# Narrower value columns, fewer GpSimd masks, a rearranged start and new scheduling durations in a fused attention and SwiGLU kernel

## The chip, the cores and the metric

The kernel runs on one core of one Trainium2 chip. The metric is the device time of one launch in microseconds; several launches are timed and the median is quoted. In the profile PE is TensorE's matmuls, PEld its weight loads (they overlap PE), DVE is VectorE, ACT is ScalarE, POOL is GpSimd and SP is the engine that issues most DMAs. "L380" is line 380 of that kernel. Line numbers differ between kernels, so the text says each time what the line does.

## The reference, cut to what matters

```python
# q, k, v: (8 batches, 8 heads, 576, 64) float32; tau = 0.02
scores = q @ k.T / 8
thresh = max(scores, axis=-1) - tau
scores = where(scores >= thresh, scores, -1e9)
attn   = softmax(scores)
x      = (attn @ v) laid out as 4608 tokens x 512
xn     = x / rms(x) * rms_g
out    = (silu(xn @ w_gate) * (xn @ w_val)) @ w_out      # 512 -> 1536 -> 512
```

The outer shapes make 144 attention steps: 36 chunks of 128 queries (32 from one batch each, 4 built from the 64 left-over queries of two batches) times 4 pairs of heads. A step computes 128 x 576 scores for two heads.

## The kernel before

One Python function builds a list of operations with their dependencies, engine and an assumed duration. A list scheduler then sorts them, and each engine executes its own list strictly in that order.

```python
COST = dict(s_main=1080.0, ..., av_main=600.0, ..., mask_g=800.0, take_g=1400.0, ..., xn=400.0, ...)   # ns
```

A step goes through these stages (cuts marked with dots):

```python
# 1. scores: TensorE, fp32, two heads side by side into PSUM
# 2. per head, VectorE: copy to SBUF and take the row minimum (scores are negated)
nc.vector.tensor_tensor_reduce(out=ssb[a][:, h], in0=s_ps[h][:, 448:1024], in1=zrow, ..., accum_out=mx[m][:, h:h + 1])
# 3. GpSimd: threshold = minimum + tau, a 128 x 2 instruction
nc.gpsimd.tensor_scalar(out=nth[m], in0=mx[m], scalar1=tau, ...)
# 4. per head one of two ways, by WAYS[s % len(WAYS)]
#    "p": ScalarE alone: a steep leaky ReLU that throws out what is over the threshold, then exp
nc.scalar.activation(out=ssb[a][:, h], in_=ssb[a][:, h], func=PRELU, scale=-1.0, bias=nth[m][:, h:h + 1], ...)
nc.scalar.activation(out=wsb[s % NW][:, h], in_=ssb[a][:, h], func=AF.Exp)
#    "g": exp on ScalarE, mask and multiply on GpSimd
nc.scalar.activation(out=esb[es], in_=ssb[a][:, h], func=AF.Exp, scale=-1.0, bias=nth[m][:, h:h + 1])
nc.gpsimd.tensor_scalar(out=wsb[s % NW][:, h], in0=ssb[a][:, h], scalar1=nth[m][:, h:h + 1], op0=ALU.is_le, ...)
nc.gpsimd.tensor_tensor(out=wsb[s % NW][:, h], in0=wsb[s % NW][:, h], in1=esb[es], op=ALU.mult)
# 5. transpose the 128 x 1152 weights by DMA (fp16)
nc.sync.dma_start_transpose(out=wt[s % NWT], in_=wsb[s % NW]...)
# 6. attention times value ("AV"): 10 matmuls; the moving side is 64 values and 64 ones
#    (a strided view over the value tile), and column 64 is the softmax sum
nc.tensor.matmul(ot[:, cs], w[:, 4 * h + j], v_rhs(b % 2, p, 5 * h + j), start=(j == 0), stop=(j == 4))
```

In this kernel `FIRST = 16` and `WAYS = ("pg",)`: the first 16 steps use ScalarE alone, and from there every second head is masked on GpSimd.

The FFN works on groups of up to four chunks. Its gate and value weights come in 24 pieces of 128 x 512, are multiplied by `rms_g` and cast to fp16 on GpSimd, and the first FFN matmul waits for all 24:

```python
for d in range(4):                                   # 128 rows
    for w_dram, w_sb in ((moe_w_gate, wg), (moe_w_val, wv)):
        for c in range(DFF // 512):                  # 512 columns
            ...
            nc.gpsimd.tensor_scalar(out=w_sb[d][:, 512 * c:512 * (c + 1)], in0=stage[slot],
                                    scalar1=rmsg[:, d:d + 1], scalar2=None, op0=ALU.mult)
...
g = add("PE", mm, pr, xops + w_done + ..., gmm, ring="R")     # w_done: all 24 casts
```

Of the kernel before, what the change touches and what calls it, by code (L numbers as in the profile page):

```python
# [13 lines left out]
SEM = 150.0  # L14
COST = dict(
    s_main=1080.0, s_virt=2160.0, tr4=480.0, av_main=600.0, av_virt=800.0, ffn4=216.0,
    ttr=850.0, evac_qk=620.0, evac_kt=420.0, prelu=740.0, exp0=660.0, exp1=750.0, mask_d=910.0, mask_g=800.0, take_g=1400.0,
    rz=120.0, xmul=400.0, sq=720.0, xn=400.0, pool_tiny=380.0, pool_dma=1300.0, sp=70.0,
    gate=0.0,
# [3 lines left out]
class Op:  # L23
    __slots__ = ("eng", "cost", "prio", "deps", "fn", "ring", "frees", "slot", "end", "start", "dma", "opens")

    def __init__(self, eng, cost, prio, deps, fn, ring=None, frees=None, dma=0.0):
        self.eng, self.cost, self.prio, self.fn = eng, cost, prio, fn
        self.deps = [d for d in deps if d is not None]
        self.ring, self.frees, self.dma = ring, frees, dma
        self.slot = self.end = self.start = None  # L30
        self.opens = ()


def order_ops(ops, ring_sizes):
# [20 lines left out]
    while len(out) < len(ops):  # L55
        best = None
        for e, lst in pending.items():
            if not lst:
                continue
            t0 = eng_free[e]  # L60
            cand = None
            for i in lst:
                o = ops[i]
                t = max(t0, ready_at[i])
                if o.ring is not None:
                    if not ring_free[o.ring]:
                        continue
                    t = max(t, min(ring_free[o.ring])[0])
                k = (t, o.prio, i)
                if cand is None or k < cand:  # L70
                    cand = k
            if cand is not None and (best is None or cand < best[0]):
                best = (cand, e)
# [3 lines left out]
        if o.ring is not None:  # L77
            got = min(ring_free[o.ring])
            ring_free[o.ring].remove(got)
            o.slot = got[1]  # L80
# [6 lines left out]
        if o.frees is not None:  # L87
            ring_free[o.frees.ring].append((o.end + SEM, o.frees.slot))
# [14 lines left out]
def kernel(  # L103
# [32 lines left out]
    id32 = sb("id32", [128, 128])  # L136
    zrow = sb("zrow", [128, S], FP16)
# [5 lines left out]
    qn = [sb(f"qn{i}", [128, 4, 2, D]) for i in range(2)]  # L143
    kn = [sb(f"kn{i}", [128, 4, 2, D]) for i in range(2)]
    qtl = [sb(f"qtl{i}", [128, H, D]) for i in range(2)]
    ktl = [sb(f"ktl{i}", [128, H, D]) for i in range(2)]
    qT = [[sb(f"qT{i}_{p}", [128, MAIN]) for p in range(NP)] for i in range(2)]
    kT = [[sb(f"kT{i}_{p}", [128, MAIN]) for p in range(NP)] for i in range(2)]
    kTt = [sb(f"kTt{i}", [128, NP, TAIL]) for i in range(2)]
    qTv = [sb(f"qTv{i}", [128, NP, 128]) for i in range(2)]  # L150
    va = [sb(f"va{i}", [128, NP, 13, D], FP16) for i in range(2)]

    def v_rhs(i, p, j):
        kind = {4: 11, 5: 12}.get(j, 10)
        a = va[i][:, p, j:j + 2]
        return bass.AP(tensor=a.tensor, offset=a.offset, ap=[a.ap[0], [D * (kind - j), 2], a.ap[2]])

# [21 lines left out]
    sl = [sb(f"sl{i}", [128, 512]) for i in range(NT_)]  # L179
    NHF = 18  # L180
# [37 lines left out]
    n_load = {"q": 0, "k": 0}  # L218
    tr_of = {"q": [], "k": []}
    k_ready = {}  # L220
    kt_ready = {}
    q_ready = {}
# [4 lines left out]
    def setup():  # L227
        o_id = add("POOL", 2000.0, -100, [], lambda o: make_identity(nc, id32))

        def consts(o):  # L230
            nc.vector.memset(zrow, 0.0)
            nc.vector.memset(mhalf, -0.5)

        def vconst(o):
            for i in range(2):
                nc.vector.memset(va[i][:, :, 10:13], 1.0)
                for j in (4, 11):
                    nc.vector.memset(va[i][64:128, :, j], 0.0)
                for j in (5, 12):
                    nc.vector.memset(va[i][0:64, :, j], 0.0)  # L240

        o_c = add("DVE", 300.0, -100, [], consts)
# [8 lines left out]
    def emit_qk(b, p, which, prio):  # L251
        nat = (qn if which == "q" else kn)
        dst = (qT if which == "q" else kT)[b % 2][p]
        src = (q if which == "q" else k)[b, 2 * p:2 * p + 2, 0:MAIN]
        n = n_load[which]
        n_load[which] += 1
        slot = n % 2
        before = [tr_of[which][n - 2]] if n >= 2 else []

        def load(o):  # L260
            for h in range(2):
                nc.sync.dma_start(out=nat[slot][:, :, h], in_=src[h].rearrange("(si sc) d -> si sc d", sc=4))

        def tr(o):
            for sc in range(4):
                nc.tensor.transpose(ring[o.slot][:, 128 * sc:128 * (sc + 1)], nat[slot][:, sc].rearrange("s h d -> s (h d)"), id32)  # L266

        lo = gated(add("SP", 70.0, prio - 3, before, load, dma=1500.0), prio - 3)
        t = add("PE", COST["tr4"], prio, [lo, o_id] + last_s.get((which, b - 2, p), []), tr, ring="R")
        tr_of[which].append(t)  # L270

        def ev(o):
            nc.scalar.activation(out=dst, in_=ring[t.slot], func=AF.Copy, scale=-0.125 if which == "q" else 1.0)  # L273

        e = add("ACT", COST["evac_qk"], prio, [t], ev, frees=t)
        (q_ready if which == "q" else k_ready)[b, p] = e

    def emit_tail_load(b, prio):
        i, e = divmod(b, 2)
        before = [x for x in tail_load.get(("use", i - 2), [])]  # L280
        for which, dst, src in (("q", qtl, q), ("k", ktl, k)):
# [3 lines left out]
            tail_load[which, b] = gated(add("SP", 70.0, prio - 3, before, load, dma=800.0), prio - 3)  # L285

    def emit_k_tail(b, prio):
        i, e = divmod(b, 2)

        def tr(o):  # L290
            for p in range(NP):
                nc.tensor.transpose(
                    ring[o.slot][:, 64 * p:64 * (p + 1)],
# [6 lines left out]
        def ev(o):  # L300
            nc.scalar.copy(out=kTt[b % 2], in_=ring[t.slot][:, 0:64 * NP].rearrange("p (a n) -> p a n", n=TAIL))

        kt_ready[b] = add("ACT", COST["evac_kt"], prio, [t], ev, frees=t)
        tail_load.setdefault(("use", i), []).append(t)

    def emit_q_tail(i, prio):
        def tr(o):
            for p in range(NP):
                nc.tensor.transpose(
                    ring[o.slot][:, 128 * p:128 * (p + 1)],  # L310
# [6 lines left out]
        def ev(o):  # L317
            nc.scalar.activation(out=qTv[i % 2], in_=ring[t.slot].rearrange("p (a n) -> p a n", n=128),
                                 func=AF.Copy, scale=-0.125)

        qv_ready[i] = add("ACT", COST["evac_qk"], prio, [t], ev, frees=t)
        tail_load.setdefault(("use", i), []).append(t)

    def emit_v(b, prio):
        t = va[b % 2]
        hv = v[b].rearrange("(a e) s d -> e s a d", e=2)
        main = v[b, :, 0:MAIN].rearrange("(a e) (si sc) d -> e si a (sc d)", e=2, sc=4)
# [8 lines left out]
        def run(lo, hi, p, j, n):  # L336
            return t[lo:hi, p:p + 2, j:j + n].rearrange("s a j d -> s a (j d)")

        for g in range(NP // 2):
            prs = [2 * g, 2 * g + 1]  # L340
            put(prs, 4 * g, run(64, 128, 2 * g, 0, 4), main[0, 0:64, prs[0]:prs[0] + 2], 360.0)
            put(prs, 4 * g + 0.1, run(0, 64, 2 * g, 1, 4), main[0, 64:128, prs[0]:prs[0] + 2], 360.0)
            put(prs, 4 * g + 0.2, run(0, 128, 2 * g, 6, 4), main[1, :, prs[0]:prs[0] + 2], 720.0)
            if g == 0:
                allp = list(range(NP))
                put(allp, 0.3, t[0:64, :, 0], hv[0, MAIN:S], 500.0)
                put(allp, 0.4, t[64:128, :, 5], hv[1, MAIN:S], 500.0)

    def emit_batch_inputs(b):
        base = first_step[b - 1] if b else -10  # L350
        emit_tail_load(b, base + (0 if b else 1))
        for p in range(NP):
            pr = base + 3.5 * p + (1.5 if b else 0)
            emit_qk(b, p, "k", pr)
            emit_qk(b, p, "q", pr + 0.1)
            if p == 0:
                emit_k_tail(b, pr + 0.2)
        emit_v(b, base + (5 if b else 0))
        if b % 2:
            emit_q_tail(b // 2, base + 13)  # L360
# [7 lines left out]
    w_dma = {}  # L368

    def emit_s(s):  # L370
        ci, p = steps[s]
        kind, b, c = chunks[ci]
        if kind == "m":
            deps = [q_ready[b, p], k_ready[b, p], kt_ready[b]]

            def fn(o):
                for lo, n, src in ((512, MAIN, kT[b % 2][p]), (448, TAIL, kTt[b % 2][:, p])):
                    for h in range(2):
                        hs = slice(64 * h, 64 * h + 64)
                        nc.tensor.matmul(s_ps[h][:, lo:lo + n], qT[b % 2][p][hs, 128 * c:128 * (c + 1)],  # L380
                                         src[hs], start=True, stop=True)
        else:
            deps = [qv_ready[b]]
            for e in range(2):
                deps += [k_ready[2 * b + e, p], kt_ready[2 * b + e]]
# [12 lines left out]
        if kind == "m":  # L398
            last_s[("q", b, p)] = [o]
            last_s[("k", b, p)] = [o] + ([last_s["k", b, p][0]] if False else [])  # L400
# [7 lines left out]
    def emit_softmax(s, so):  # L408
# [3 lines left out]
        for h in range(2):  # L412
            def ttr(o, h=h):
                nc.vector.tensor_tensor_reduce(  # L414
                    out=ssb[a][:, h], in0=s_ps[h][:, 448:1024], in1=zrow, scale=1.0, scalar=3.0e38,
# [8 lines left out]
        wfree = [w_dma.get(s - NW)]  # L424
        done = []
        for h in range(2):
            way = (WAYS[s % len(WAYS)] if s >= FIRST else "pp")[h]
            if way == "p":
# [7 lines left out]
                pl = add("ACT", COST["prelu"], s + 0.5, [tn], prelu)  # L436
                done.append(add("ACT", COST["exp0"], s + 0.5, [pl] + wfree, ex))
# [34 lines left out]
        def tdma(o):  # L472
            nc.sync.dma_start_transpose(out=wt[s % NWT], in_=wsb[s % NW].rearrange("p h s -> p (h s)"))

        w_dma[s] = add("SP", COST["sp"], s, done + [av_of.get(s - NWT)], tdma, dma=1700.0)

    def emit_av(s):
        ci, p = steps[s]
        kind, b, c = chunks[ci]
        col = (s % 2) * 4 * D  # L480
        w = wt[s % NWT]

        def fn(o):
            for h in range(2):
                cs = slice(col + h * 2 * D, col + (h + 1) * 2 * D)
                if kind == "m":
                    for j in range(5):
                        nc.tensor.matmul(ot[:, cs], w[:, 4 * h + j], v_rhs(b % 2, p, 5 * h + j),  # L488
                                         start=(j == 0), stop=(j == 4))
                else:  # L490
                    for e in range(2):
                        for j in range(5):
                            nc.tensor.matmul(ot[64 * e:64 * e + 64, cs], w[:, 4 * h + j, 64 * e:64 * e + 64],  # L493
                                             v_rhs(e, p, 5 * h + j), start=(j == 0), stop=(j == 4))

        bs = [b] if kind == "m" else [2 * b, 2 * b + 1]
        deps = [w_dma[s]] + [x for bb in bs for x in v_ready[bb, p]]
# [3 lines left out]
        av_of[s] = o  # L501
# [4 lines left out]
    def emit_half(s):  # L506
# [4 lines left out]
        o3 = ot.rearrange("p (h d) -> p h d", d=2 * D)  # L511
# [248 lines left out]
```

## Time and profile before

| | before |
|---|---|
| time, median (all runs beside the changed kernel) | 704.02 us (701.69 to 707.34) |
| span of the profiled run | 699.8 us |
| TensorE, GpSimd, ScalarE, VectorE busy | 92, 76, 65, 61% |
| first FFN matmul starts at | 90.7 us |

I cut the span at two landmarks that can be read from the timeline of TensorE. The first is the start of the scores of step 20, after the first batch and the first left-over chunk; the second is the end of the last scores. This gives a start, a middle and a tail that hold the same attention work in every kernel. (The amount of FFN work ahead of a landmark differs. Counted in matmuls of the full 512 columns, 0.215 us each, 18 lie ahead of the first landmark in the kernel before. Behind the second they are 202.) These are the three stretches of the kernel before; the columns are the stretch, its length, busy us and instruction count of PE, PEld, DVE, ACT and POOL, then granted clock, DMA share and GB/s:

```profile
0.00:99.10 99.10, 72.02 (x455) 47.58 (x455) 39.89 (x116) 61.13 (x102) 63.80 (x79) 0.85 1.02 193
99.10:645.70 546.60, 521.32 (x3953) 305.26 (x3952) 357.05 (x866) 372.32 (x629) 458.20 (x484) 0.98 0.67 123
645.70:699.80 54.10, 48.46 (x463) 35.76 (x459) 31.86 (x102) 21.79 (x58) 7.33 (x9) 1.00 0.21 52
```

In the start TensorE is idle for 27 us, at a granted clock of 0.85, and the DMA engines are full. In the middle TensorE is 95% busy and GpSimd 84%. The chain of waits of the whole span, by engine, has both:

```profile
PE 45%; POOL 29%; issue 8%; DMA 6%; ACT 6%; DVE 4%; SPq 1%; POOLq 0%; DVEq 0%; ACTq 0%
```

### The profile page before, as it was taken

Reading aid. Unit: us, or ns where it says so; the run is one execution under the profiler, and the core shown is the slowest. Engines: PE = TensorE matmul, PEld = TensorE weight load, DVE = VectorE, ACT = ScalarE, POOL = GpSimd, SP = SyncE. Lnnn points to the kernel's source line nnn. Section 1 sums busy time; section 2 is a strip of 40 time slices with the busy share of each in tenths; the row PEclk is TensorE's granted clock in tenths of the full one; section 3 lists DMA queues with packets and bytes.
Section 4 is the critical chain, followed back from the end, with each engine's and each line's share of the span. In section 5 each row is a group of like instructions: output and inputs, shape, how many; then the busy total and the mean of one; then the engine's idle time right before and its main releaser. Section 6 shows DMA issues by size and latency. Waiting matters only on the chain.

```text
span 699.8 us, 13808 instructions
## 1 busy us (share of the span) xinstructions
PE 641.8 (92%) x4864; PEld 388.6 (56%) x4864; DVE 428.8 (61%) x1080; ACT 455.2 (65%) x789; POOL 529.3 (76%) x570
## 2 busy tenths in 40 slices
PE   5787699989899898999999999999999989999997
PEld 3455466756545444555675545555555544556775
DVE  2353465754568645875685784767478656865654
ACT  2867566666767656766776866776677756766443
POOL 3087987599889966898898987899789977887300
PEclk9897889998899999999999999999999999999999
DMA  9899997487686546975897455977596454444410
GB/s 163 172 257 202 214 145 159 76 138 136 139 119 115 98 107 133 145 124 122 171 129 144 91 114 116 162 119 124 118 183 114 85 107 101 78 97 112 82 46 31
DMA packets 290325, 89.00 MB, mean 127 GB/s; under 512 B 272848, under 2 KB 282576, under 8 KB 290256
## 3 DMA queue, kind: packets, MB, share of 16 engines
q1 hardware_dynamic: 275344, 81.83, 59.1%
q0 software_dynamic: 14912, 6.30, 8.7%
q8 instruction: 38, 0.62, 0.4%
q14 instruction: 31, 0.25, 0.1%
HBM read 37.75 MB, written 9.44 MB: 67 GB/s over the span
## 4 chain that ended last, share of the span: by engine, by line
PE 45%; POOL 29%; issue 8%; DMA 6%; ACT 6%; DVE 4%; SPq 1%; POOLq 0%; DVEq 0%; ACTq 0%
POOL wsb L457 13%; PE s_ps L380 12%; POOL wsb L462 8%; PE ring L615 8%; PE ring L576 6%; PE ring L581 6%; DMA wt<-wsb 5%; PE ot L488 5%; POOL nth L421 2%; ACT ssb L430 2%; DVE ssb L414 2%; PE ring L266 2%; PE ot L493 2%; POOL wv L674 2%; ACT wsb L434 1%
## 5 line engine op out<-in xcount | busy, mean ns | idle before, releaser
L414 DVE CUSTOM_DVE_ANT_0 ssb<-s_ps,zrow 128x576 f32<-128x576 f32 x288 | 208.4, 753 | 135.8 <-PE s_ps L380 91.9
L457 POOL TENSOR_SCALAR wsb<-ssb,nth 128x576 f16<-128x576 f32 x128 | 221.6, 1731 | 9.1
L380 PE MATMUL s_ps<-kT,qT 64*128 64x512 f32 x512 | 172.3, 676 | 15.0 <-DVE mx L414 9.9
L462 POOL TENSOR_TENSOR wsb<-wsb,esb 128x576 f16<-128x576 f16 x128 | 163.4, 1277 | 11.3 <-ACT esb L443 1.9
L443 ACT ACTIVATE esb<-ssb,nth 128x576 f16<-128x576 f32 x128 | 98.8, 772 | 95.0 <-POOL nth L421 94.6
L430 ACT ACTIVATE ssb<-ssb,nth 128x576 f32<-128x576 f32 x160 | 121.0, 762 | 12.4 <-POOL nth L421 12.4
L581 PE MATMUL ring<-xnT,wv 128*128 128x512 f16 (+2 forms) x528 | 108.4, 328 | 2.6 <-DVE sl L591 1.8
L488 PE MATMUL ot<-va,wt 128*128 128x128 f16 x1280 | 97.4, 226 | 14.6 <-DMA wt<-wsb 12.0
L434 ACT ACTIVATE wsb<-ssb 128x576 f16<-128x576 f32 x160 | 107.6, 680 | 3.9
L576 PE MATMUL ring<-xnT,wg 128*128 128x512 f16 (+2 forms) x520 | 107.3, 329 | 0.9 <-ACT qT L273 0.7
L588 ACT ACTIVATE th<-ring 128x512 f32<-128x512 f32 (+2 forms) x130 | 63.0, 488 | 57.2 <-PE ring L576 57.0
L488 PEld LDWEIGHTS <-wt 128*128 128x128 f16 x1280 | 80.3, 101 | 34.8 <-DMA wt<-wsb 21.8
L591 DVE SCALAR_TENSOR_TENSOR sl<-th,ring 128x512 f32<-128x512 f32 (+2 forms) x130 | 71.9, 553 | 45.1 <-ACT th L588 43.1
L421 POOL TENSOR_SCALAR nth<-mx 128x2 f32<-128x2 f32 x144 | 34.6, 240 | 81.6 <-DVE mx L414 61.6
L380 PEld LDWEIGHTS s_ps<-kTt,qT 64*128 64x128 f32 x512 | 62.3, 196 | 60.3 <-issue 58.5
L615 PE MATMUL ring<-wo,hf 128*128 128x512 f16 x396 | 90.3, 379 | 0.0
L596 DVE TENSOR_TENSOR hf<-ring,sl 128x512 f16<-128x512 f32 (+2 forms) x132 | 73.7, 558 | 12.1 <-PE ring L581 2.4
L380 PEld LDWEIGHTS s_ps<-kT,qT 64*128 64x128 f32 x512 | 48.8, 194 | 57.3 <-DVE mx L414 26.5
L581 PEld LDWEIGHTS <-wv 128*128 128x128 f16 x624 | 54.6, 98 | 33.4 <-issue 4.6
L576 PEld LDWEIGHTS <-wg 128*128 128x128 f16 x624 | 55.2, 98 | 31.4 <-issue 1.7
L615 PEld LDWEIGHTS <-hf 128*128 128x128 f16 x432 | 40.7, 98 | 44.9 <-issue 0.2
L380 PE MATMUL s_ps<-kTt,qT 64*128 64x64 f32 x512 | 54.0, 252 | 0.0
(50 smaller groups left out, 515.9 us busy)
## 6 DMA issues: line engine op xcount, KB each, us to landing
kn<-in_k_dram SPq DMA_DIRECT2D x64, 128.0 KB, 3.1
qn<-in_q_dram SPq DMA_DIRECT2D x64, 128.0 KB, 3.5
out_dram<-osb SPq DMA_DIRECT2D x32, 256.0 KB, 2.6
th<-in_moe_w_gate_dram SPq DMA_DIRECT2D x12, 256.0 KB, 3.5
sl<-in_moe_w_val_dram SPq DMA_DIRECT2D x12, 256.0 KB, 3.6
wt<-wsb SPq DMA_TRANSPOSE x144, 3.3
va<-in_v_dram POOLq DMA_DIRECT2D x32, 64.0 KB, 4.0
va<-in_v_dram POOLq DMA_DIRECT2D x16, 128.0 KB, 4.5
```

What stands on the lines that cost most here:

```text
L380: nc.tensor.matmul(s_ps[h][:, lo:lo + n], qT[b % 2][p][hs, 128 * c:128 * (c + 1)], src[hs], start=True, stop=True)
L414: nc.vector.tensor_tensor_reduce(out=ssb[a][:, h], in0=s_ps[h][:, 448:1024], in1=zrow, scale=1.0, scalar=3.0e38, op0=ALU.add, op1=ALU.min, ...
L430: nc.scalar.activation(out=ssb[a][:, h], in_=ssb[a][:, h], func=PRELU, scale=-1.0, bias=nth[m][:, h:h + 1], **PRELU_KW)
L434: nc.scalar.activation(out=wsb[s % NW][:, h], in_=ssb[a][:, h], func=AF.Exp)
L443: nc.scalar.activation(out=esb[es], in_=ssb[a][:, h], func=AF.Exp, scale=-1.0, bias=nth[m][:, h:h + 1])
L457: nc.gpsimd.tensor_scalar(out=wsb[s % NW][:, h], in0=ssb[a][:, h], scalar1=nth[m][:, h:h + 1], scalar2=None, op0=ALU.is_le)
L462: nc.gpsimd.tensor_tensor(out=wsb[s % NW][:, h], in0=wsb[s % NW][:, h], in1=esb[es], op=ALU.mult)
L488: nc.tensor.matmul(ot[:, cs], w[:, 4 * h + j], v_rhs(b % 2, p, 5 * h + j), start=(j == 0), stop=(j == 4))
L576: nc.tensor.matmul(ring[o.slot][:, 0:n], wg[d][:, fs], xnT[slot][:, d, 0:n], start=(d == 0), stop=(d == 3))
L581: nc.tensor.matmul(ring[o.slot][:, 0:n], wv[d][:, fs], xnT[slot][:, d, 0:n], start=(d == 0), stop=(d == 3))
L596: nc.vector.tensor_tensor(out=hf[hi][:, 0:n], in0=ring[vv.slot][:, 0:n], in1=sl[i][:, 0:n], op=ALU.mult)
L615: nc.tensor.matmul(ring[o.slot], hf[hs[fc][0]][:, 128 * j:128 * (j + 1)], wo[:, fc], start=(fc == 0), stop=(fc == NFC - 1))
```

## The change

The intent is to give TensorE less to do, to take GpSimd off the path, and to get through the start sooner. The diff, cut to its core (cuts are marked with "..."; helpers for two PSUM slots per operation, renamed tiles, merged q/k tiles, four staging tiles of their own for the weight loads, output weights that no longer wait for casts, and other priorities are left out):

```diff
-    s_main=1080.0, s_virt=2160.0, tr4=480.0, av_main=600.0, av_virt=800.0, ffn4=216.0,
-    ttr=850.0, ..., mask_g=800.0, take_g=1400.0,
+    s_main=1120.0, s_virt=1130.0, tr4=480.0, tr8=560.0, av_main=360.0, av_virt=500.0, ffn4=216.0,
+    ttr=690.0, ..., mask_g=1740.0, take_g=1300.0,
...
-    va = [sb(f"va{i}", [128, NP, 13, D], FP16) for i in range(2)]
+    va = [sb(f"va{i}", [128, NP, 10, D + 1], FP16) for i in range(2)]
...
-            put(prs, 4 * g, run(64, 128, 2 * g, 0, 4), main[0, 0:64, prs[0]:prs[0] + 2], 360.0)
+            put([p], VSTEP[b > 0] * p, t[64:128, p, 0:4, 0:D], main[2 * p, 0:64], 500.0)
...
-                        nc.tensor.matmul(ot[:, cs], w[:, 4 * h + j], v_rhs(b % 2, p, 5 * h + j),
+                        nc.tensor.matmul(ot[:, cs], w[:, 4 * h + j], va[b % 2][:, p, 5 * h + j],
...
+        if s < N_PE:
+            def tr(o):
+                for j in range(9):
+                    nc.tensor.transpose(ring[...], wsb[s % NW][... 128 * j:128 * j + 128], id16)
+            ...                       # and two copies PSUM -> wt on VectorE
+        else:
             nc.sync.dma_start_transpose(out=wt[s % NWT], in_=wsb[s % NW]...)
...
-            nc.vector.tensor_scalar(out=xn[ci % 2], in0=xsb[ci % 2], scalar1=ir[i3], scalar2=None, op0=ALU.mult)
+            nc.gpsimd.tensor_scalar(out=xn[ci % 2], in0=xsb[ci % 2], scalar1=ir[i3], scalar2=1.0,
+                                    op0=ALU.mult, op1=ALU.mult)
...
-    for d in range(4):
-        for w_dram, w_sb in ((moe_w_gate, wg), (moe_w_val, wv)):
-            for c in range(DFF // 512):
+    for c in range(DFF // 512):
+        for d in range(4):
+            for w_dram, w_sb in ((moe_w_gate, wg), (moe_w_val, wv)):
...
-                    nc.gpsimd.tensor_scalar(
+                    nc.vector.tensor_scalar(          # the cast of the weights
...
-FIRST = 16
-WAYS = ("pg",)
+FIRST = 0
+WAYS = ("pg", "pp")
+N_PE = 16
+EVAC = ("ACT", "DVE")                                 # k^T now leaves PSUM by VectorE
```

A value tile now holds 64 values and one column of ones per block, so the loads write rows of 64 values with a gap, where two heads' worth of four blocks went as runs of 256 values before. `WAYS = ("pg", "pp")` masks one head in four on GpSimd, and `N_PE = 16` is the number of first steps whose weights TensorE transposes. An FFN matmul now waits only for the 8 casts of its own column block. Where both heads of a step go the "p" way, one exp covers both.

## The prediction

> **What bounds the kernel now.** I read the page first (engine shares, slices), then one table of five stretches of the span, then the chain that ended last in two of them.
>
> ```profile
> PE 641.8 (92%) x4864; PEld 388.6 (56%) x4864; DVE 428.8 (61%) x1080; ACT 455.2 (65%) x789; POOL 529.3 (76%) x570
> ...
> PE   5787699989899898999999999999999989999997
> ...
> POOL 3087987599889966898898987899789977887300
> PEclk9897889998899999999999999999999999999999
> DMA  9899997487686546975897455977596454444410
> ```
>
> TensorE is the fullest engine, GpSimd the second. The PE row is low only in the first six or seven slices (about 100 us); there DMA is at 9 and the granted clock below full.
>
> The stretches (us, length, busy us and instructions of PE, PEld, DVE, ACT, POOL, then clock, DMA share, GB/s):
>
> ```profile
> 0.00:20.00 20.00, 10.74 (x52) 7.62 (x52) 5.81 (x20) 6.20 (x10) 6.47 (x16) 1.00 1.06 161
> 20.00:100.00 80.00, 62.19 (x406) 40.71 (x408) 34.87 (x98) 55.75 (x95) 58.23 (x63) 0.81 1.01 201
> 100.00:340.00 240.00, 224.09 (x1709) 135.44 (x1706) 148.46 (x372) 159.41 (x274) 201.21 (x214) 0.96 0.70 127
> 340.00:640.00 300.00, 290.62 (x2188) 164.78 (x2188) 202.49 (x479) 208.44 (x348) 251.73 (x266) 1.00 0.65 120
> 640.00:700.00 60.00, 54.16 (x514) 40.05 (x512) 37.16 (x114) 25.45 (x66) 11.69 (x14) 1.00 0.23 56
> ```
>
> So PE is 73% busy to 100 us (72.9 of 100), 93% to 340, 97% to 640, 90% in the tail. A busy PE still counts pipeline ends, so I add the work from start-to-start times of the timeline: scores 1.23 us a step (144 steps, 178 us), FFN matmuls 0.86 us per four of 512 columns and 2.59 us per twelve of the output (280 us in all), the q/k transposes about 32 us, attention-times-value (AV) 56 ns each (below), 1600 of them, 90 us. Sum 580 of 700 us; some 120 us are lost. Before 100 us only about 20 of 144 score steps and five of the twelve column blocks of the first FFN group are done, some 47 us of work, so 53 us are lost there; 13 us go in the tail (47 us of work in 60), and some 55 between 100 and 640.
>
> What takes them is in the chain of 20 to 100 us and of 340 to 400 us:
>
> ```profile
> 43.63 3.11 POOL wv L674 x2
> ...
> 70.86 3.10 POOL wg L674 x2
> ...
> 82.24 3.11 POOL wg L674 x2
> ```
>
> ```profile
> 342.53 0.52 POOL wsb L462
> 343.05 0.85 issue
> 343.90 0.23 POOL nth L421
> 344.22 1.74 POOL wsb L457
> 346.03 1.28 POOL wsb L462
> ```
>
> Early, the threshold (L421) of every step waits in GpSimd's in-order queue behind weight casts (L674, 24 of 1.57 us). Later, in stretches, mask plus multiply plus threshold, 1.74+1.28+0.23 = 3.25 us, are the step's pace; in others (354 to 385 us) the chain is PE alone.
>
> **What the Trainium skill says.**
> (1) "TensorE: Matmul & The Clock Gate", section "Back-to-back issue gap": an isolated warm gap is N/2.4 + 2.5 ns, so 56 ns at N=128, but about 81 ns sustained with weight loads. This trace:
>
> ```profile
> 304.53 0.72 PE L488 MATMUL ot<-va,wt 128*128 128x128 f16 x10
> 305.09 1.03 PE L576 MATMUL ring<-xnT,wg 128*128 128x512 f16 x4
> ```
>
> 0.56 us for ten load-and-matmul pairs, 56 ns: the loads are hidden, the first figure holds here and the second doesn't. At 65 columns the formula gives 29.6 ns; whether loads still hide is not shown.
> (2) "GPSIMD Engine Reference", section "Elementwise — side-by-side cycle accounting": two-input work about 2.6 cycles an element at 1.2 GHz. L462: 1277 ns for 576 is 2.66; it agrees. The mask at 1731 ns (3.6 cycles) is dearer than its one-input figure.
> (3) "SBUF — State Buffer", "shared port pair" among its terms: VectorE in a two-port mode and GpSimd lock one pair exclusively and the loser waits. The normalise on VectorE (L534) has 479/520/1500 ns min/median/max; that spread agrees, and its mean is 819.
> (4) "ScalarE: Activation LUTs", "What ACT_TABLE_LOAD costs": 186 ns + 0.833 ns an element without a pointer operand: 666 ns at 576, the trace has 680; 1146 at 1152.
>
> **The change part by part.**
> *AV with 65 columns.* 1600 matmuls, from 56 ns to somewhere from 30 (stream bound) to 56 (load bound). I choose 36: minus 20 ns x 1600 = 32 us, nearly all between 100 and 640 us where PE is the bound. On the path, about 30 us.
> *Masks on every fourth head.* L457 and L462 fall from 128 to 72: minus 56 x (1.731+1.277) = minus 168 us of GpSimd. ACT: prelu from 160 to 216 (+56 x 0.762 = +43), biased exp from 128 to 72 (-43), 160 exps of 0.68 (109) become 72 of 0.68 and 72 double ones of about 1.15 (132, +23). The k copy out of PSUM goes to DVE (-19). ACT ends near 460 us, no bound.
> *Casts to DVE.* GpSimd minus 37 us; DVE plus 24 x (0.5 to 1.5, as L534) = about 20.
> *Normalise to GpSimd.* Plus 36 x 1.57 (the cast's row, same shape) = at most 56; DVE minus 29.
> *Value loads.* One row of 64 per descriptor, 112 loads for 96: GpSimd plus 16 x 0.67 = 11. GpSimd ends at 529-168-37+56+11 = about 390 us, near 60%.
> *First 16 steps' transposes on PE.* 144 x about 60 ns = plus 9 us of PE and 32 DVE copies of about 0.45 us (14 us), while PE is a quarter idle; in return 16 transposing DMAs leave the crowded start, and their landing (3.3 us median) leaves the latency of a step. DVE ends near 428+19+20-29+14 = 452, no bound.
> *Weights by column block.* The first FFN matmul waits for 8 casts, not 24. In the instruction order it comes after 16 score steps, before after 19: the gain is less the order than that nothing waits for the last cast at 90 us.
>
> The sum by stretch. *To 100 us:* of the 80 us from 20 to 100 the chain gives L674 23%, about 19 us; that leaves, ACT's part (20%) shrinks a little with masks on GpSimd, 9 us of transposes come into idle PE, the value loads take some back: minus 18. *100 to 640:* minus 30 of AV, and of the 55 us lost some 15, since GpSimd per step falls from 3.7 to about 2.7 us while PE's work is near 3.9. The rest of the 55 is the fixed in-order interleaving and stays. *Tail:* the order leaves about as many FFN columns behind the last score step (34,816 per projection for 32,768): minus 0. In all minus 63, from 706: **643 us**.
>
> **Rivals.**
> *DMA becomes the bound.* The software queue has 14,912 packets at 8.7% of 16 engines' 700 us, 65 ns each. With one packet per 64 values, the value rows go from 1536 to 4608 a batch, +24,600 in all: 24,600 x 65/16 = +100 us of every engine's time; 16 transposes of about 1.7 us leave (-27). DMA share goes from 68% to about 85% of 643 us, and it's already full before 100 us. For it: landing of wt is 5% of the chain. Against: in the middle it is 0.65 to 0.70, buffers are five deep, and the small packets may be cheaper. If it bites: 665 to 685.
> *Weight loads bind AV.* Then the 32 us shrink to under 10 and the time is about 665. For it: each load shows 101 ns. Against: ten overlapped in 0.56 us.
> *DVE/GpSimd port fights.* Casts on DVE beside GpSimd masks from step 0 delay the score reductions (L414, 753 ns x2 a step), which free the score PSUM. Costs at most the 18 us gained early: 660.
> *A better fit than I allow.* With PE left as the only bound and interleaving much better the 55 us halve again: about 620.
>
> **Range and chances.** AV term 10 to 40 us, start 0 to 25, GpSimd relief 5 to 30, DMA 0 to -25: the centre is 643, eight in ten lie from 616 to 676. Slower than 692 needs nearly all terms to fail at once. Faster 0.94, same 0.05, slower 0.01.
>
> **What would show it.** AV bursts of ten in 0.30 to 0.40 us (56 ns kept: step wrong). POOL near 390 us and gone from the chain after 100 us; PE at 95% or more, with near 615 us busy. First FFN matmul before 80 us (90.7 now), and the start stretch shorter by 10 to 25 us. wt landing still near 3.3 us; if 5 or more and waits of PE for wt grow beyond the present 43 us, the DMA rival holds. What would make it wrong: a PE no busier than now, with waits for DVE or for wt in place of GpSimd's.

## The result, and the profile after

The changed kernel takes 637.95 us (635.67 to 640.57, 4 runs) beside 704.02 us of the kernel before. The ratio is 0.906, with a 95% interval of 0.900 to 0.912. Ratios here and below are the mean time of one kernel's fast runs over the mean of the other's fast runs of the same rounds, so they are not quite the ratio of the medians quoted.

The engines and slices of the changed kernel, from its page:

```profile
PE 602.6 (95%) x5008; PEld 362.5 (57%) x5008; DVE 441.3 (69%) x1129; ACT 461.5 (73%) x741; POOL 382.3 (60%) x518
...
PE   5799979997999999999999999999999999998996
...
POOL 4799565758495745966785654876396744653000
PEclk9999979999799999999999999999999999999999
DMA  9999876887798556987896549997797553445100
```

TensorE has 39 us less busy time and a larger share; it is at 9 from the third slice on almost without a break. GpSimd fell from 76 to 60%. The chain of waits by engine has lost GpSimd:

```profile
PE 79%; DVE 8%; DMA 4%; issue 3%; POOL 3%; ACT 2%; SPq 0%; DVEq 0%; POOLq 0%; ACTq 0%
```

The three stretches between the same landmarks, in the same columns as before:

```profile
0.00:83.50 83.50, 69.26 (x626) 48.04 (x626) 65.88 (x175) 54.67 (x83) 59.49 (x85) 1.00 0.95 167
83.50:578.30 494.80, 483.98 (x3906) 277.67 (x3902) 344.07 (x855) 384.33 (x599) 318.17 (x429) 0.98 0.74 137
578.30:635.60 57.30, 49.38 (x482) 36.75 (x481) 31.39 (x100) 22.49 (x60) 4.63 (x6) 1.00 0.18 46
```

The start is 15.6 us shorter, the middle 51.8 us and the tail 3.2 us longer, together 64.2 us of span. The middle's TensorE is 98% busy, 10.8 us short of full where it was 25.3 us short.

An AV burst and what follows it on TensorE, from the timeline:

```profile
43.23 0.49 PE L511 MATMUL ot<-va,wt 128*128 128x65 f16 x10
43.56 0.66 PE L480 MATMUL ring<-id,wsb 128*128 128x128 f16 x9
```

The next instruction starts 0.33 us after the burst's start, so a matmul of 65 columns takes 33 ns with its weight load, where one of 128 took 56.

### The profile page after: what moved, and what is told of

Its sections match the earlier page's. It is cut to its first block, busy times and chain, and to the rows that moved or that the text cites. A ratio compares the mean times of both kernels' runs of the same rounds, so it can differ in the third digit from the quotient of the medians.

```text
span 635.6 us, 13838 instructions
## 1 busy us (share of the span) xinstructions
PE 602.6 (95%) x5008; PEld 362.5 (57%) x5008; DVE 441.3 (69%) x1129; ACT 461.5 (73%) x741; POOL 382.3 (60%) x518
## 3 DMA queue, kind: packets, MB, share of 16 engines
q1 hardware_dynamic: 256400, 77.11, 57.8%
q0 software_dynamic: 40256, 6.30, 13.5%
## 4 chain that ended last, share of the span: by engine, by line
PE 79%; DVE 8%; DMA 4%; issue 3%; POOL 3%; ACT 2%; SPq 0%; DVEq 0%; POOLq 0%; ACTq 0%
PE s_ps L377 24%; PE ring L641 12%; PE ring L605 12%; PE ring L600 12%; PE ot L511 6%; PE ring L264 4%; DVE ssb L410 3%; DMA wt<-wsb 3%; PE s_ps L389 2%; PE s_ps L641 2%; PE ot L516 1%; POOL wsb L461 1%; DVE sl L617 1%; DVE hf L622 1%; PE s_ps L600 1%
## 5 line engine op out<-in xcount | busy, mean ns | idle before, releaser
L428 ACT ACTIVATE ssb<-ssb,nth 128x576 f32<-128x576 f32 x216 | 159.1, 765 | 49.0 <-POOL nth L417 48.4
L377 PE MATMUL s_ps<-qkT 64*128 64x512 f32 x512 | 172.4, 658 | 8.2 <-DVE mx L410 5.7
L461 POOL TENSOR_SCALAR wsb<-ssb,nth 128x576 f16<-128x576 f32 x72 | 124.9, 1735 | 9.4 <-PE ring L480 3.7
L377 PEld LDWEIGHTS s_ps<-kTt,qkT 64*128 64x128 f32 x512 | 63.8, 192 | 57.2 <-issue 54.9
L466 POOL TENSOR_TENSOR wsb<-wsb,esb 128x576 f16<-128x576 f16 x72 | 92.3, 1281 | 5.6
L435 ACT ACTIVATE wsb<-ssb 128x1152 f16<-128x1152 f32 x72 | 83.7, 1162 | 4.8 <-DMA wt<-wsb 1.5
L333 POOL DMA_DIRECT2D va<-in_v_dram x112 | 77.2, 694 | 2.7 <-PE s_ps L377 0.6
L377 PEld LDWEIGHTS s_ps<-qkT 64*128 64x128 f32 x512 | 51.1, 189 | 46.9 <-DVE mx L410 24.6
L511 PE MATMUL ot<-va,wt 128*128 128x65 f16 x1280 | 62.0, 195 | 5.8 <-DMA wt<-wsb 4.9
L447 ACT ACTIVATE esb<-ssb,nth 128x576 f16<-128x576 f32 x72 | 55.4, 770 | 15.7 <-POOL nth L417 15.5
```

The lines of the kernel that those rows point to most:

```text
L377: nc.tensor.matmul(s_ps[h][:, lo:lo + n], qkT[b % 2][p][hs, c], src[hs], start=True, stop=True)
L435: nc.scalar.activation(out=wsb[s % NW], in_=ssb[a], func=AF.Exp)
L511: nc.tensor.matmul(ot[:, cs], w[:, 4 * h + j], va[b % 2][:, p, 5 * h + j], start=(j == 0), stop=(j == 4))
```

## The experiments

Twelve kernels were run, all correct, each beside the kernel before on the same chip (runs 1 to 4, 5 to 8 and 9 to 12 on three chips, on which the kernel before took 702.6, 703.4 and 703.4 us). Start, middle and tail of each, in us:

| kernel | time | ratio to before | start | middle | tail |
|---|---|---|---|---|---|
| before | 704.0 | 1 | 99.1 | 546.6 | 54.1 |
| changed | 638.0 | 0.906 | 83.5 | 494.8 | 57.3 |
| 1. changed, 128 columns | 660.7 | 0.940 | 84.4 | 515.7 | 57.7 |
| 2. before, 65 columns | 720.5 | 1.025 | 108.1 | 557.0 | 53.2 |
| 3. changed, masks on every second head | 690.7 | 0.982 | 84.2 | 547.5 | 56.7 |
| 4. before, masks on every fourth head | 702.2 | 0.999 | 113.8 | 531.1 | 58.1 |
| 5. changed, no TensorE transposes | 664.3 | 0.944 | 108.4 | 491.6 | 57.3 |
| 6. changed, weights by row block | 634.4 | 0.902 | 78.0 | 499.2 | 57.2 |
| 7. changed, casts on GpSimd | 660.6 | 0.940 | 119.7 | 484.8 | 57.2 |
| 8. before, new order | 679.8 | 0.969 | 96.3 | 527.4 | 55.4 |
| 9. changed, old durations | 643.4 | 0.915 | 90.1 | 495.7 | 54.8 |
| 10. before, new order, GpSimd relieved | 672.6 | 0.957 | 102.3 | 510.7 | 55.8 |
| 11. as 10, 65 columns | 666.7 | 0.947 | 112.6 | 497.9 | 56.1 |
| 12. changed, by row block, 20 steps on TensorE | 628.2 | 0.894 | 77.8 | 493.1 | 57.9 |

The time is the median, the stretches are from the profiled run, and the "before" row is the kernel before as it ran beside the changed kernel. A profiled run can lie some us from its median (run 5's was 5 us faster, run 7's 3 us slower), so a difference of a few us between stretches is within the noise. Where the list of operations or their durations differ, the instruction order is made anew as well; of the runs that undo or add a part, only run 1 keeps its order.

Two theories stood at first. Theory A is the prediction's: after the change TensorE is the bound, so its savings are worth nearly their full length, while before it GpSimd hid part of them. Theory B says that GpSimd's relief made the gain and TensorE's saving is idle.

### 1 and 2: the columns, undone and alone

```diff
 # 1, in the changed kernel: the next block is streamed too and never read
-    nc.tensor.matmul(ot[:, cs], w[:, 4 * h + j], va[b % 2][:, p, 5 * h + j], ...)
+    nc.tensor.matmul(ot[:, cs], w[:, 4 * h + j], va_flat[b % 2][:, p][:, 65 * j:65 * j + 128], ...)
 # 2, in the kernel before: layout, value loads and AV matmuls of the changed kernel
-    va = [sb(f"va{i}", [128, NP, 13, D], FP16) for i in range(2)]
+    va = [sb(f"va{i}", [128, NP, 10, D + 1], FP16) for i in range(2)]
```

(The code line of run 1 is written out short; it takes columns 65(5h+j) to 65(5h+j)+127 of the flattened tile, which has one more block of zeros at its end.)

> The changed kernel with 128 value columns streamed for 65 (the 63 more are the next block's, never read), everything else and the instruction order as it is. AV bursts of ten go from 0.33 back to 0.56 us. Theory A (TensorE is the bound after the change, so its time is worth its full length): 1280 x 23 ns + 320 x 8 ns = 32 us come back, about 665 to 672 us. Rival B (GpSimd's relief made the gain, TensorE has slack beside it): under 10 us more, below 648 us.

> The kernel before with the 65-column layout, value loads and AV matmuls of the changed kernel, nothing else. Theory A: before, GpSimd's 3.25 us a step sets the pace in stretches and hides part of TensorE's saving, so only 10 to 20 us of the 32 show: 684 to 694 us. If TensorE's length is worth its whole length there too: about 672. Rival B: 700 or more. If the small value packets hurt: slower than before, with wt landing later than 3.3 us.

Run 1 took 660.7 us, 22.7 us more than the changed kernel; 20.9 of these lie in the middle, where some 1,100 AV matmuls of 23 ns make about 25 us:

```profile
84.40:600.10 515.70, 508.52 (x3903) 301.53 (x3902) 344.35 (x853) 386.68 (x599) 317.10 (x429) 0.99 0.73 131
```

The instruction counts are those of the changed kernel within 3. So with GpSimd relieved, most of the columns' saving is on the path, but not all of it. Theory B's bound of 10 us is broken; my 27 to 34 us were too many.

Run 2 became slower than the kernel before, by 2.5% (interval 1.020 to 1.031). This is its start and middle:

```profile
0.00:108.10 108.10, 75.69 (x464) 50.04 (x464) 39.26 (x114) 61.20 (x103) 72.62 (x91) 0.78 1.07 180
108.10:665.10 557.00, 507.37 (x3937) 288.53 (x3936) 353.66 (x862) 371.23 (x628) 484.32 (x522) 0.95 0.67 120
```

TensorE is busy for 14 us less in the middle than before (507 for 521), yet the middle is 10 us longer. GpSimd went from 458 to 484 us there: over the whole kernel it issues 112 value loads of 0.68 us, 48 more than before. In the start it issues more too, and the granted clock fell from 0.85 to 0.78 (in the middle from 0.98 to 0.95). That GpSimd's added time is the cause fits, but isn't shown. The sign for harm by the packets, weight tiles landing later than 3.3 us, did not come: their median is 2.9 us. And a rival stands untested: the old table takes a value load for 1.30 us, about twice the measured 0.68, so the 48 more of them also change the order, which run 8 shows to matter. Run 11 comes back to the loads.

### 3 and 4: the masks, undone and alone

```diff
 # 3, in the changed kernel
-FIRST = 0
-WAYS = ("pg", "pp")
+FIRST = 16
+WAYS = ("pg",)
 # 4, in the kernel before: the opposite
```

> The changed kernel with GpSimd masks on every second head again from step 16, none before (the instruction order is made anew). GpSimd near 382 + 56 x 3.0 = 550 us busy. Theory A: 15 to 25 us slower, 653 to 663 us, with GpSimd back in the chain. Rival B: 40 us or more slower, 678 or more.

> The kernel before with GpSimd masks on every fourth head from step 0, nothing else (the order is made anew, from the old cost table). GpSimd near 360 us busy. Theory A: 15 to 25 us faster, 680 to 690 us. Rival B: 45 us faster or more, 660 or less.

Run 3 lost 52.8 us, twice what theory A allowed and in the range of rival B (678 us or more), all of it in the middle. GpSimd is busy for 500.5 of its 547.5 us:

```profile
84.20:631.70 547.50, 510.47 (x3893) 292.69 (x3892) 345.57 (x856) 358.83 (x598) 500.49 (x551) 0.94 0.69 123
```

The changed kernel has moved the normalise (25 us) and 48 loads onto GpSimd, so the old mask share brings it to 91% busy, and its part of the chain of waits is 19% for the changed kernel's 3%. TensorE's own busy time in the middle grew too, 510.5 for 484.0 us, at a granted clock of 0.94 for 0.98; how much of the loss goes with the clock is not separated. That the moves would be a mistake without fewer masks is likely; no run makes them alone.

Run 4 gained nothing (0.999, interval 0.995 to 1.004). The table shows where it went: its middle is 15.5 us shorter, as theory A expected of the whole, and its start 14.7 us longer. The likely reason is that the masks of the first steps now queue with the weight casts in GpSimd:

```profile
0.00:113.80 113.80, 80.84 (x470) 54.12 (x470) 41.80 (x121) 58.25 (x97) 86.80 (x95) 0.78 0.93 174
```

GpSimd is busy for 86.8 us of this start where it was 63.8 us. So neither theory holds as written: run 1 broke B's bound, run 3 met B's figure and not A's, and run 4 met neither.

### 5, 6 and 7: the parts of the start, undone

```diff
 # 5
-N_PE = 16
+N_PE = 0
 # 6: the loop order of the kernel before, and each FFN matmul waits for all 24 casts
-    for c in range(DFF // 512):
-        for d in range(4):
-            for w_dram, w_sb in ((moe_w_gate, wg), (moe_w_val, wv)):
+    for d in range(4):
+        for w_dram, w_sb in ((moe_w_gate, wg), (moe_w_val, wv)):
+            for c in range(DFF // 512):
 # 7
-                    nc.vector.tensor_scalar(          # the cast
+                    nc.gpsimd.tensor_scalar(
```

> The changed kernel with all 144 weight transposes by DMA again. TensorE loses 144 small transposes (11 us of its busy time, up to 100 us) and DVE 32 copies. My theory: in the start they fill idle TensorE, and 16 transposing DMAs of about 1.7 us return to a crowded queue: step 20 starts at 90 to 95 us (83.5 in the changed kernel), the whole 5 to 12 us slower, 643 to 650 us. Rival: TensorE's 11 us are on the path, then the kernel gets faster, 628 to 635 us.

> The changed kernel with gate and value weights loaded row block by row block, all 24 casts ahead of the first FFN matmul; casts stay on DVE. First FFN matmul near 90 us (65.0 in the changed kernel). My theory: less FFN work is done early and has to be done later by a TensorE that is full: 5 to 10 us slower, 643 to 648 us. Rival: only what leaves GpSimd counts and the order of the loads nothing: within 3 us of 638.

> The changed kernel with the 24 weight casts on GpSimd at 1.57 us each (the order is made anew with that cost). My theory: thresholds and masks queue behind them until about 90 us, the start is 15 to 20 us longer and the time 650 to 658 us. Rival: with masks on every fourth head GpSimd has room for 38 us, under 5 us slower.

Run 5 lost 26 us, 24.9 of span in the start, two to five times my 5 to 12. (Its profiled run is the fastest of its four, so the span shows only 21.7 us more.) The stretch from 20 to 100 us in the changed kernel, the same in run 5, and one piece of run 5's chain:

```profile
20.00:100.00 80.00, 72.41 (x664) 49.78 (x665) 69.28 (x183) 56.85 (x88) 56.86 (x75) 0.96 0.85 166
...
20.00:100.00 80.00, 60.23 (x352) 39.85 (x353) 41.08 (x105) 41.47 (x65) 47.69 (x63) 0.72 1.10 182
...
79.34 10.39 DMA wt<-wsb
```

In the changed kernel TensorE is busy for 72.4 us of that stretch at a clock of 0.96 and a DMA share of 0.85; here it is 60.2 us at 0.72 and 1.10. One transposed tile was on the chain for 10.4 us, and the slowest landing was 13.3 us, where the changed kernel's slowest is 6.9. Late tiles and the lower clock come together; which share each has of the 25 us is not separated.

Run 6 shows no gain from the order of the weight loads. The first FFN matmul slid from 65.0 to 100.2 us, the start got 5.5 us shorter and the middle 4.4 us longer, and the time is 634.4 us: ratio 0.902 with an interval of 0.897 to 0.906, which overlaps the changed kernel's. In the stretches, FFN work done early delays the first attention steps by about as much as it relieves later ones. My expected 5 to 10 us did not come; the rival's "within 3 us" was missed by 0.6, on the fast side.

Run 7 lost 22.6 us. Its stretch from 20 to 100 us has a nearly full GpSimd and DMA engines that are idle for a good part, probably because in the program a staging tile is free for the next load only after its cast:

```profile
20.00:100.00 80.00, 63.71 (x487) 44.27 (x488) 44.04 (x118) 40.61 (x65) 74.00 (x76) 0.81 0.60 119
```

The start became 36 us longer, and 10 of it came back in the middle, where 42 fewer full-width FFN matmuls were left, about 9 us.

### 8 and 9: the order alone

The new durations change no instruction of a given kernel, only which goes first (and with it which PSUM slot an operation is given). Run 8 gives the kernel before a table of durations near those of its own trace; run 9 gives the changed kernel the old table.

```diff
 # 8, in the kernel before
-    ttr=850.0, ..., mask_d=910.0, mask_g=800.0, take_g=1400.0, ...
+    ttr=690.0, ..., mask_d=750.0, mask_g=1740.0, take_g=1300.0, ...     # and casts 1570 for 900
 # 9, in the changed kernel: the old values
```

> The kernel before, the same instructions with the same operands, but ordered by durations measured in its own trace (TensorE scores 1.12, DVE reductions 0.69, GpSimd masks 1.74, casts 1.57 us and so on) in place of the old table. My theory: GpSimd's load sets the pace in stretches whatever the order: 697 to 707 us. Rival: the better order is itself a main part of the gain: 675 to 690 us.

> The changed kernel ordered by the old table of durations (GpSimd mask 0.80 for the 1.73 us measured, DVE reduction 0.85, normalise on GpSimd 0.40 and so on); instructions and operands the same. If the order is worth as much here as the 23 us it gave the kernel before: 655 to 665 us. If it mattered only because GpSimd was crowded: within 8 us of 638, since GpSimd has slack now.

Run 8 is the surprise: 679.8 us, ratio 0.969 (0.963 to 0.975), with the same instructions. My theory, that GpSimd sets the pace whatever the order, fell; the rival held. GpSimd's busy time is the same (529.9 for 529.3 us), and the middle is 19 us shorter with TensorE fuller:

```profile
96.30:623.70 527.40, 512.41 (x3934) 303.51 (x3932) 349.02 (x864) 371.80 (x628) 461.45 (x487) 0.99 0.70 127
...
PE 55%; POOL 21%; issue 7%; DMA 7%; DVE 4%; ACT 3%; SPq 2%; DVEq 0%; POOLq 0%; ACTq 0%
```

GpSimd's part of the chain fell from 29 to 21%. The old table took a GpSimd mask for 0.80 us, where it takes 1.73, so other engines' lists were built around results that came a microsecond late. That this entry, of all that changed, is the one that counts was not tested.

Run 9 is only 5.5 us slower than the changed kernel, and its middle is the same (495.7 for 494.8 us). With slack on GpSimd the wrong durations matter little; what is lost is in the start, 90.1 for 83.5 us. The gains of order and of the other parts therefore overlap: the order is worth 24 us where it comes first and 5.5 where it comes last, and the two must not be added.

### 10 and 11: building up from the kernel before

```diff
 # 10, in the kernel of run 8
-FIRST = 16
-WAYS = ("pg",)
+FIRST = 0
+WAYS = ("pg", "pp")
-                    nc.gpsimd.tensor_scalar(          # the cast
+                    nc.vector.tensor_scalar(
 # 11: also the 65-column layout, as in run 2
```

> The kernel before in the new order (679.8 us), with masks on every fourth head from step 0 and the casts on DVE: GpSimd near 325 us busy. Alone the masks gave nothing (their start was 15 us longer, behind the casts). If the two parts complete each other: start 90 to 95 us, middle about 510 us, together 650 to 662 us. If they don't: 675 or more.

> The one before, with the 65 column layout and its value loads as well. With GpSimd out of the way TensorE's saving should show as it did in the changed kernel: 18 to 25 us faster than the one before. If the value loads' packets or their GpSimd time were what made the kernel before slower with 65 columns, it gains under 8 us or loses.

In run 10 the middle came to 510.7 us, as expected (510), 17 us less than in run 8, of which about 4 are FFN work that moved into the start. The start did not get shorter: 102.3 us, not 90 to 95, and the time is 672.6, not 650 to 662. The start is not quite as bad as it looks: 30 more full-width FFN matmuls lie in it than in the kernel before, about 6 us, and by step 28 the scores start at 136.1 us, where they start at 142.9 in the kernel before.

Run 11 is 5.9 us faster than run 10: not the 18 to 25 of my theory, and inside the other case, under 8 us if the value loads did the harm. The stretches say where it goes. The middle is 12.8 us shorter, and the start 10.3 us longer (the two profiled spans differ by only 2.2 us, so a few us of this are noise):

```profile
0.00:102.30 102.30, 79.22 (x528) 52.93 (x528) 57.17 (x157) 61.10 (x104) 51.95 (x72) 0.88 1.03 197
102.30:613.00 510.70, 501.03 (x3874) 297.00 (x3872) 340.62 (x849) 405.69 (x683) 271.04 (x359) 1.00 0.71 129
```

```profile
0.00:112.60 112.60, 85.92 (x494) 54.22 (x494) 53.40 (x146) 59.83 (x100) 57.54 (x81) 0.76 1.09 180
112.60:610.50 497.90, 484.92 (x3893) 276.71 (x3892) 340.70 (x854) 405.80 (x685) 299.37 (x397) 0.99 0.74 132
```

The first is run 10, the second run 11. Three times as many value packets enter DMA engines that were full already (1.03, then 1.09), the bandwidth falls from 197 to 180 GB/s, and the granted clock from 0.88 to 0.76. GpSimd is busy for 5.6 us more there as well, and the order is made anew. So a part of the prediction's DMA rival is likely real, but only in the start; packets, GpSimd time and order were not taken apart. The changed kernel takes 16 transposing DMAs out of this start, and its start is 29 us shorter than run 11's. Run 5 shows 25 us for these transposes alone, taken out of the changed kernel.

### 12: an attempt to beat both

```diff
 # the kernel of run 6
-N_PE = 16
+N_PE = 20
```

> The changed kernel with weights by row block and 20 in place of 16 steps transposed on TensorE, an attempt to beat it: the crowded start lasts to step 20. Expected 628 to 636 us if the start gains 3 us or more, 638 to 642 if the 36 further transposes (2 to 3 us of a full TensorE) are all that changes.

It took 628.2 us (627.1 to 631.1, 5 runs), ratio 0.894 with an interval of 0.891 to 0.897, clear of the changed kernel's 0.900 to 0.912, and inside my 628 to 636. It is the fastest kernel here, about 1.3% ahead (0.894 over 0.906). The start equals run 6's and the middle is 6 us shorter; the four more steps on TensorE lie at that landmark, and the stretch just behind it is the one that benefits: the scores of step 28 start at 107.9 us for run 6's 115.2, and the lead is 6 us at the end of the scores. The granted clock from 78 to 120 us is 0.92 for 0.84. Why that stretch gains more than a microsecond a step is not shown.

## Why the prediction was right or wrong, point by point

**The sum held, in part by luck.** 643 us was predicted (63 off the 706 then known), 638.0 measured, within the range of 616 to 676 and faster as given 0.94. But on the path the AV term was 9 to 17 us too large, and the order, worth 17 to 19 us in the middle, was not in the sum. Two of the three stretches came close: the start 15.6 us shorter for 18, the middle 51.8 for 45. The tail grew by 3.2 us for 0; its six more full-width FFN matmuls are about 1.3 of these.

**What was right.** TensorE as the bound after the change: 95% of the span (602.6 us busy, near 615 expected), 79% of the chain, GpSimd down to 3% of it. AV bursts of ten in 0.33 us, inside the 0.30 to 0.40 asked for, and 33 ns for the 36 chosen: 1280 x 23 ns is 29 us of the 32 before the left-over chunks are counted. The first FFN matmul at 65.0 us, under the 80 given. Transposed tiles landing after 3.2 us, and TensorE's waits for them down from 43 to 12 us (waits of weight loads and of matmuls added, though they overlap; those of matmuls alone fell from 16.2 to 5.2), so the DMA rival did not bite in the whole. The double exp took 1.16 us for 1.15. The rival of the shared port did not show at the score reductions either, 753 ns on average before and after; that it caused the spread of the normalise was not tested. ScalarE ended at 461.5 us for 460, GpSimd at 382.3 for 390, VectorE at 441.3 for 452.

**The AV term was mis-sized on the path.** The step "On the path, about 30 us" should have read 13 to 21: 20.9 us in the middle of run 1, where everything else is relieved, and 12.8 in the middle of runs 10 and 11, whose value loads differ too. The matmuls' own saving was as computed, but the middle had 10.8 us of other waits even in the changed kernel, and a shorter TensorE probably meets them sooner.

**The order was wrongly called fixed.** "The rest of the 55 is the fixed in-order interleaving and stays" is the step that failed. Run 8 takes 19 us out of the middle of the kernel before by reordering alone. I had read the new table of durations in the diff as bookkeeping. In the middle, in the order in which I built it up, the gain is 19 us for order, 17 for masks and casts, 13 for the columns with their loads and 3 for the rest (546.6, 527.4, 510.7, 497.9, 494.8); with the FFN work that moved across the landmarks taken off, about 17, 13, 12 and 5. Taken in another order the parts would differ, as run 9 shows with order last: 1 us.

**The start's gain had another cause.** The prediction gave it to the casts (19 us in the chain) and charged the transposes on TensorE with their cost. Runs 5 and 7 show that both are needed: without the transposes on TensorE the start is 25 us longer, without the casts on VectorE 36. They do not add either. Run 10, which has the casts and masks but not the transposes, has no shorter start than the kernel before, though with about 6 us more FFN work in it.

**The column blocks of the weights** were rated low, and showed no worth by themselves (run 6).

**Errors that cancelled in GpSimd's sum.** I wrote 112 value loads for 96; the page has 64 before, so the term was +34 us for my 11 (77.2 for 42.9 us). The normalise on GpSimd was taken for 56 us from the cast's row and took 25.1. The small packets were taken for 65 ns each; the software queue shows 13.5% of 16 engines over 635.6 us for 40,256 packets, 34 ns each, and the DMA share ended at 72% for the expected 85. The 1.7 us of a transposing DMA is the program's assumed duration, read from no trace: in run 5 the hardware queue takes 62.0% of 657.3 us, 57.8% of 635.6 in the changed kernel, 40 us more for the 16, so about 2.5 us each.

## What to carry to other kernels

When several engines run in-order lists near their limits, undo a part from the new kernel and add it alone to the old one: here the columns and the masks were worth 23 and 53 us taken out, and minus 18 and nothing put in. Look, too, at how much other work crosses a landmark before comparing stretches. Before shortening anything, check that the durations which the schedule is built from are the measured ones; that alone gave a third of this gain, without touching an instruction. In a start that is limited by DMA, moving transposes onto an idle TensorE can pay: here the start was 25 us shorter with it, at a DMA share of 0.95 for 1.11 and a granted clock of 1.00 for 0.80. Which of the two brings the gain, and whether the clock is cause or effect, is not shown.

## What the Trainium skill lacked or had wrong

- "TensorE: Matmul & The Clock Gate", section "Back-to-back issue gap", gives about 81 ns a matmul at N=128 when weight loads are interleaved. Here it was 56 ns with loads, in bursts of ten, and 33 ns at 65 columns, 3 ns over what its isolated-gap formula gives.
- "GPSIMD Engine Reference", section "Elementwise — side-by-side cycle accounting", has no figure that tells two forms of one instruction apart: a 128 x 512 float32 to fp16 multiply by a per-partition scalar took 1.57 us with one operation (the weight cast of the kernel before) and 0.70 us with a second, a multiply by 1.0 (the normalise of the changed kernel). Run 7 has both in one kernel, at 1.57 and 0.69 us, but on different tiles, and no run swaps the forms, so that the form is the cause is not shown.
- No page that I read says what many small packets cost beside transposing DMAs in full queues: a transposed tile that lands in 3.2 us (median) took up to 13.3 us in run 5 (6.9 in the changed kernel), and the start of run 11, with three times the value packets, was 10 us longer than run 10's.
